# The low parts of a next batch's keys and values are formed by GpSimd instead of VectorE

## The chip, the cores and the metric

The kernel runs on one core of a Trainium2 chip. The metric is the device time of one execution in microseconds (us). A core has five engines that run side by side, each its own list of instructions in order, and wait for each other by semaphores: TensorE (PE in the profile, with PEld for its weight loads), VectorE (DVE), ScalarE (ACT), GpSimd (POOL) and SyncE (SP), which here only issues transfers (DMA).

## The reference

Two stages: an attention with squared ReLU in the place of a softmax, and a mixture of experts of which each token uses one.

```
scores = (1 / S) * z @ z.T                      # per batch: 2496 x 64 -> 2496 x 2496
attn   = max(scores, 0) ** 2
x      = u * (attn @ v)                         # v, u: 8 x 2496 x 256
...
do_compute = x @ w_skip > 0
xc     = x[do_compute]
logits = xc @ w_gate                            # 8 experts
e_idx  = argmax(logits)
gate_w = softmax(logits)[e_idx]
y      = gate_w * (max(xc @ w1[e_idx], 0) @ w2[e_idx])    # 256 -> 1024 -> 256
out    = x;  out[do_compute] = xc + y
```

All data are float32.

## The kernel before

**High and low parts.** TensorE multiplies in a rounded format (`F32R`). To keep the accuracy of float32 each factor is split: the high part is the rounded copy, the low part is what the rounding lost (`low = x - high`), and a product is three matmuls, high by high, high by low and low by high. So there are `zh`, `zl` for the queries and keys, `vh`, `vl` for the values, and `ah`, `al` for the squared scores.

**Loads.** `load_z` (L100) brings a tile `zf` of 128 x 512 of the transposed z by a DMA on SyncE, and returns a function that forms the parts: ScalarE casts `zh` (L108), and the engine that was passed in as `eng` subtracts for `zl` (L109). `load_v` (L113) does the same for a group of 256 rows of v: `raw`, then `vh` (L119) and `vl` (L120) of 128 x 512. There are four raw tiles, three `zf`, 35 tiles for `vh` and `vl` and seven each for `zh` and `zl`. A batch has ten groups of v and five tiles of z.

**Steps.** A batch is cut into five chunks of queries: four of 512 (`QC`) and a last of 448. For every chunk the loop goes through ten groups of 256 keys, in the order of `ORDER`. One (chunk, group) is a step; eight batches make 400 steps. `stage(s + LA)` with `LA` = 2 prepares the step two ahead: TensorE computes scores (L251), ScalarE applies ReLU (L292) and squares (L293), ScalarE or VectorE rounds to `ah` (L315), and VectorE subtracts for `al` (L319). Then `attend` (L346) multiplies `ah` and `al` with `vh` and `vl`, into accumulators `acc`. Because scores are symmetric, some tiles of squared scores are turned by VectorE (L268), kept in DRAM (`kept`) and read back in a later step in place of being computed again; in the last chunk such a tile comes as three pieces for `ah` and `al`.

At the end of a chunk VectorE adds and multiplies (L376, L379) and turns the result (L383), and it is stored. After every second chunk comes a routing: logits on TensorE (L414), on VectorE a series of small operations that choose the expert (L447 to L456), count the tokens (L460 to L468) and later form the places (L487 to L503), and on GpSimd indirect DMAs that scatter the tokens' ids into lists (L505).

**Order.** The order on every engine is written out by hand: `at(s, f)` puts `f` behind the work of step `s // 2` (so `s` counts half steps), and `later(s, k, load, ...)` starts the transfer at `s` and forms the parts `k` half steps later. While batch b is computed, `jobs` places the loads of batch b + 1: each entry is (function, group, chunk, position in the chunk), the transfer starts 3.5 steps before the position.

**The experts.** After the attention, weights are loaded in the same way by `load_w`; for all experts but the first the subtractions run on GpSimd already (L151, L157). Tokens are fetched by indirect DMAs (L556), multiplied, and put out (L654).

Of the kernel before, what the change touches and what calls it, by code (L numbers as in the profile page):

```python
# [47 lines left out]
def attn_moe(ctx, tc, zT, uT, v, wg, w1, w2, cst, pad, out):  # L48
# [4 lines left out]
    nc = tc.nc  # L53
# [3 lines left out]
    NB = v.shape[2]  # L57
# [105 lines left out]
    def load_u(ci):  # L163
        b, q0, n = chunks[ci]
        uts[ci] = xp.tile([P, 2, QC], F32, name="ut", tag="ut", bufs=3)
        nc.sync.dma_start(uts[ci][:, :, :n], uT[b, :, :, q0 : q0 + n])
# [509 lines left out]
    def at(s, f):  # L676

        todo.setdefault(s // 2, []).append(f)
# [24 lines left out]
    def later(s, k, load, *args):  # L703
        def start():
            f = load(*args)
            at(s + k, f)
        at(s, start)

    for ci, (b, q0, n) in enumerate(chunks):
        s0 = ci * NB  # L710
        if ci + 1 < NC:
            at(s0 + 12, lambda ci=ci: load_u(ci + 1))
        if ci == 0:
            first = [(4 * j - 8, j % 2, 3, load_z, j) for j in range(2, NZ)]
            first += [(2 * g - 4, 1, 4, load_v, g) for g in range(2, NB // 2)]
            for s1, _, k, load, j in sorted(first, key=lambda x: x[:2]):
                eng = nc.vector
                if s1 - k < 0:
                    at(s1, load(0, j, eng))
                else:  # L720
                    later(s1 - k, k, load, 0, j, eng)
            at(14, lay_pads)
        if q0 == 0 and b + 1 < B:

            jobs = [(load_v, 0, 1, 3), (load_z, 0, 1, 6), (load_v, 1, 2, 3), (load_z, 1, 2, 5), (load_v, 2, 2, 7)]
            jobs += [(load_v, 3, 3, 3), (load_v, 4, 3, 4), (load_v, 5, 3, 6), (load_v, 6, 3, 7)]
            jobs += [(load_v, 7, 4, 2), (load_z, 2, 4, 3), (load_v, 8, 4, 4), (load_z, 3, 4, 5)]
            jobs += [(load_v, 9, 4, 6), (load_z, 4, 4, 7)]
            for load, j, c, k in jobs:
                later(s0 + c * NB + 2 * k - 7, 7, load, b + 1, j, nc.vector)  # L730

    s_end = NC * NB
    s_w = s_end - 3 * NB
# [27 lines left out]
    for s, (ci, p) in enumerate(steps):  # L761
        b, q0, n = chunks[ci]
        k = s % NP
# [252 lines left out]
```

## Time and profile before

| | |
|---|---|
| time, median of 3 runs | 1785.65 us (1785.43 to 1788.15) |
| profiled execution, its time | 1782.95 us |
| profiled execution, its span | 1781.2 us |
| clock granted to TensorE | 0.999 |
| busy: TensorE, weight loads | 1760.8 us, 1555.9 us |
| busy: VectorE, ScalarE, GpSimd | 1185.5 us, 1159.5 us, 446.9 us |

A span goes from the first to the last instruction. A busy time is the union of an engine's instructions in the trace. The attention takes the span's first 1280 us or so, the experts the rest. Rows of a group read: line, engine, operation, written tile <- read tiles, shapes, count, then busy us and mean ns of one, then the engine's idle time just before these instructions and what ended it. Rows in order of time read: start us, length us, engine, line, operation, tiles, shapes, count; in brackets is idle time before it and what ended it.

### The profile page before, as it was taken

What the parts mean: (1) busy time and instruction counts of PE and PEld (TensorE: products, weight loads), DVE (VectorE), ACT (ScalarE), POOL (GpSimd) and SP (SyncE); (2) the same over time, 40 slices, a digit from 0 to 9 for tenths busy, and PEclk for the clock granted to TensorE, in tenths of its full rate; (3) what the DMA queues carried; (4) which work ended last, traced back from release to release, by engine and by line L of the source; (5) the groups of instructions that cost most, each with busy time, mean ns of one, the idle gap of its engine ahead of it and who ended that gap; (6) DMA issues with size and microseconds to landing.
All of it is one profiled execution on the core that took longest, in us unless ns stands there. A gap on an engine that the chain in (4) does not pass through costs nothing.

```text
span 1781.2 us, 40579 instructions
## 1 busy us (share of the span) xinstructions
PE 1760.8 (99%) x15844; PEld 1555.9 (87%) x15844; DVE 1185.5 (67%) x2113; ACT 1159.5 (65%) x1499; POOL 446.9 (25%) x421
## 2 busy tenths in 40 slices
PE   8999999999999999999999999999999999999997
PEld 6879878987887898788889888888999999999997
DVE  6877877787887787788778778777753433343332
ACT  8878877877788777778777877877633333333321
POOL 0102201211220120121112022012255556635621
PEclk9999999999999999999999999999999999999999
DMA  5476689478857947894794789488652323313210
GB/s 190 125 181 151 158 211 223 98 200 220 177 140 193 230 104 195 213 211 109 199 219 117 189 206 222 112 191 196 158 120 76 91 84 110 95 52 90 87 38 26
DMA packets 403763, 267.44 MB, mean 150 GB/s; under 512 B 205859, under 2 KB 334117, under 8 KB 403440
## 3 DMA queue, kind: packets, MB, share of 16 engines
q1 hardware_dynamic: 389440, 240.47, 55.2%
q0 software_dynamic: 13712, 22.99, 4.6%
q8 instruction: 141, 2.31, 0.6%
q14 instruction: 182, 1.49, 0.3%
q10 hardware_dynamic: 288, 0.17, 0.0%
HBM read 145.80 MB, written 118.39 MB: 148 GB/s over the span
## 4 chain that ended last, share of the span: by engine, by line
PE 86%; DMA 4%; ACT 3%; DVE 3%; issue 2%; SPq 1%; POOL 0%; DVEq 0%; POOLq 0%; ACTq 0%
PE acc L346 52%; PE psh L605 11%; PE y L624 11%; PE ps L251 10%; DMA out<-o,idt 2%; DVE al L319 2%; DMA r<-kept 1%; ACT ah L315 1%; PE psm L414 1%; SPq L280 1%; ACT r L292 1%; ACT r L293 1%; PE pst L574 1%; DVE rt L268 0%; DMA xr<-xrow 0%
## 5 line engine op out<-in xcount | busy, mean ns | idle before, releaser
L346 PE MATMUL acc<-ah,vh 64*128 64x512 f32 (+1 forms) x3120 | 661.6, 385 | 1.3 <-DVE ah L315 1.1
L346 PE MATMUL acc<-ah,vl 64*128 64x512 f32 (+1 forms) x3120 | 644.0, 383 | 0.0
L319 DVE TENSOR_TENSOR al<-r,ah 128x1024 fp32r<-128x1024 f32 (+3 forms) x464 | 479.1, 1048 | 190.9 <-ACT ah L315 181.1
L346 PE MATMUL acc<-al,vh 64*128 64x512 f32 (+1 forms) x3120 | 514.1, 385 | 1.5 <-DVE al L319 0.9
L505 POOL DMA_INDIRECT lst<-pair,dest x160 | 198.0, 1238 | 1052.1 <-DVE dest L503 952.4
L346 PEld LDWEIGHTS acc<-ah,vh 64*128 64x128 f32 x3120 | 347.2, 184 | 56.5 <-ACT ah L315 2.8
L292 ACT ACTIVATE r<-ps 128x1024 f32<-128x1024 f32 (+1 forms) x278 | 280.1, 1007 | 178.9 <-PE ps L251 170.0
L346 PEld LDWEIGHTS acc<-ah,vl 64*128 64x128 f32 x3120 | 346.0, 184 | 50.3 <-DVE vl L120 0.2
L346 PEld LDWEIGHTS acc<-al,vh 64*128 64x128 f32 x3120 | 320.8, 184 | 59.0 <-DVE al L319 10.9
L315 ACT CAST ah<-r 128x1024 fp32r<-128x1024 f32 (+3 forms) x381 | 330.4, 892 | 51.2 <-PE acc L346 38.3
L293 ACT ACTIVATE r<-r 128x1024 f32<-128x1024 f32 (+1 forms) x278 | 289.9, 1043 | 8.8
L610 ACT ACTIVATE hh<-psh 128x512 fp32r<-128x512 f32 (+1 forms) x172 | 98.8, 583 | 286.8 <-PE psh L605 246.6
L605 PE MATMUL psh<-xt,w1h 128*128 128x256 f32 (+1 forms) x1280 | 235.1, 285 | 2.3 <-issue 1.8
L624 PE MATMUL y<-w2t,hh 128*128 128x256 f32 x1328 | 235.9, 281 | 0.0
L611 DVE SCALAR_TENSOR_TENSOR hl<-psh,hh 128x512 fp32r<-128x512 f32 (+1 forms) x172 | 113.0, 670 | 137.2 <-ACT hh L610 129.3
L624 PEld LDWEIGHTS y<-w2t,hh 128*128 128x128 f32 x1328 | 202.3, 189 | 0.6 <-issue 0.6
L605 PEld LDWEIGHTS psh<-xt,w1h 128*128 128x128 f32 x1280 | 197.4, 189 | 3.2 <-issue 3.2
L624 PE MATMUL y<-w2t,hl 128*128 128x256 f32 x664 | 184.7, 278 | 1.3 <-DVE hl L611 1.3
L605 PE MATMUL psh<-xt,w1l 128*128 128x256 f32 (+1 forms) x640 | 181.9, 284 | 0.0
L268 DVE STREAM_TRANSPOSE rt<-r 128x512 f32<-128x512 f32 x244 | 158.3, 686 | 1.6 <-DMA kept<-rt 1.5
L251 PE MATMUL ps<-zh 64*128 64x512 f32 (+1 forms) x556 | 126.0, 398 | 4.8 <-ACT zh L108 4.8
L624 PEld LDWEIGHTS y<-w2t,hl 128*128 128x128 f32 x664 | 124.7, 188 | 1.6 <-DVE hl L611 1.5
(170 smaller groups left out, 1610.3 us busy)
## 6 DMA issues: line engine op xcount, KB each, us to landing
kept<-rt SPq DMA_DIRECT2D x244, 256.0 KB
r<-kept SPq DMA_DIRECT2D x488, 128.0 KB
raw<-in_v SPq DMA_DIRECT2D x80, 256.0 KB
ut<-in_uT SPq DMA_DIRECT2D x32, 512.0 KB
xr<-xrow SPq DMA_DIRECT2D x128, 128.0 KB
out<-xrow SPq DMA_DIRECT2D x128, 128.0 KB
raw<-in_w SPq DMA_DIRECT2D x64, 256.0 KB
zf<-in_zT SPq DMA_DIRECT2D x40, 256.0 KB
```

Of the source, the lines that this page charges most:

```text
L251: nc.tensor.matmul(to, k[h, o : o + P], queries(q, h, n), start=(m == 0), stop=(m == 2))
L268: nc.vector.transpose(t[:, :, 32 * k : 32 * k + 32], r[:, x, :].rearrange("p (m i) -> p m i", i=32))
L292: nc.scalar.activation(r[:, :, :n], ps[:, :, :n], AF.Relu, scale=isc)
L293: nc.scalar.activation(r[:, :, :n], r[:, :, :n], AF.Square)
L315: (nc.scalar.copy if on_act(ci, p) else nc.vector.tensor_copy)(h_, r_)
L319: nc.vector.tensor_sub(l_, r_, f32(h_))
L346: nc.tensor.matmul(acc[t][:, :n], w[h, x, dd], a[h, x, :n], start=(first and t not in halves[:m]), stop=(last and t not in halves[m + 1 :]),)
L505: put = nc.gpsimd.indirect_dma_start(out=lst, out_offset=bass.IndirectOffsetOnAxis(ap=dest[:, t : t + 1], axis=0), in_=pair[:, t, :], in_o ...
L605: nc.tensor.matmul(ps[:, j * W : (j + 1) * W], wt[:, a, o : o + P], x[:, d, :W], start=(m == 0), stop=(m == 5),)
L610: nc.scalar.activation(hh[:, : G * W], ps[:, : G * W], AF.Relu)
L611: nc.vector.scalar_tensor_tensor(hl[:, : G * W], ps[:, : G * W], 0.0, f32(hh[:, : G * W]), op0=ALU.max, op1=ALU.subtract)
L624: nc.tensor.matmul(ys[t], h[:, tt], w2t[f][:, k, :], start=(f == 0 and m == 0 and t % 2 == 0), stop=(f == NF - 1 and m == 2), skip_group_c ...
```

## The change

In `jobs`, the loads of the next batch's z and v, the engine that subtracts is `nc.gpsimd` in place of `nc.vector`:

```diff
@@ -727,7 +727,7 @@
             jobs += [(load_v, 7, 4, 2), (load_z, 2, 4, 3), (load_v, 8, 4, 4), (load_z, 3, 4, 5)]
             jobs += [(load_v, 9, 4, 6), (load_z, 4, 4, 7)]
             for load, j, c, k in jobs:
-                later(s0 + c * NB + 2 * k - 7, 7, load, b + 1, j, nc.vector)
+                later(s0 + c * NB + 2 * k - 7, 7, load, b + 1, j, nc.gpsimd)
```

The casts to `zh` and `vh` stay on ScalarE and the transfers on SyncE, at the same steps. The first batch's loads and the first expert's weights keep VectorE. So 7 x 10 subtractions for `vl` and 7 x 5 for `zl` change their engine, at the same places of the written order.

## The prediction

> **What bounds the kernel now.** I read the page's head first, then the waits of TensorE, then the groups by shape, and last the order of time around the places where TensorE waits. The page:
>
> ```profile
> span 1781.2 us, 40579 instructions
> PE 1760.8 (99%) x15844; PEld 1555.9 (87%) x15844; DVE 1185.5 (67%) x2113; ACT 1159.5 (65%) x1499; POOL 446.9 (25%) x421
> DVE  6877877787887787788778778777753433343332
> POOL 0102201211220120121112022012255556635621
> ```
>
> The first row is the span, the second the busy time of each engine, the other two the busy tenths of VectorE and GpSimd in 40 slices of 44.5 us. TensorE is busy 99% of the span. The attention fills the first 28 to 29 slices; there VectorE is at 70 to 80% and GpSimd at 0 to 20%. So there is room to move work into, but room on VectorE is worth only what TensorE waits for it. That is in the waits of TensorE (who waited, for what, total us, times, longest):
>
> ```profile
> PEld acc L346 <- DVE al L319: 10.9, 24, 0.6
> PE acc L346 <- DVE al L319: 0.9, 5, 0.2
> ```
>
> The weight loads of the second product waited 10.9 us in all for `al`, the matmuls themselves 0.9 us. No cure of VectorE can return more than about 10.9 us, 0.6% of the span, and most of it lies inside time in which earlier matmuls still ran.
>
> **The change part by part.** It moves 7 x 15 = 105 subtractions (ten `vl`, five `zl` for each of the batches b+1 = 1 to 7, formed during b = 0 to 6) from VectorE to GpSimd. Their groups, and the like group on GpSimd from the later part of the kernel:
>
> ```profile
> L120 DVE TENSOR_TENSOR vl<-raw,vh 128x512 fp32r<-128x512 f32 x80 | 54.0, 676 | 1.5 <-ACT vh L119 1.5
> L109 DVE TENSOR_TENSOR zl<-zf,zh 128x512 fp32r<-128x512 f32 x40 | 27.3, 681 | 3.9 <-ACT zh L108 3.9
> L151 POOL TENSOR_TENSOR w1l<-raw,w1h 128x512 fp32r<-128x512 f32 x24 | 30.9, 1298 | 0.5
> ```
>
> Removed from VectorE: 105 x 0.68 = 71 us busy. Added on GpSimd: 105 x 1.30 = 136 us, in the attention, where it is mostly idle. By length alone all of this is hidden: the casts on ScalarE and the DMAs of SyncE keep their places, and the last `zl` of a batch (step 47 of 50) is first read by the scores staged in step 52, five steps of 3.2 us (1281 / 400) later, so a GpSimd that is some us late costs nothing. Queued behind a `vl` on GpSimd are only scatters into `lst` (L505), which nothing reads before the last chunk, while the last moved load is in step 347 of 400. The raw tile comes free for the next transfer up to about 1 us later; four buffers with a reuse distance of five steps cover that.
>
> What is not hidden is the meeting of GpSimd and VectorE. These rows (start, length) show it:
>
> ```profile
> 280.26 0.97 POOL L505 DMA_INDIRECT lst<-pair,dest  x1 [0.30 <-issue]
> 401.79 1.69 POOL L505 DMA_INDIRECT lst<-pair,dest  x1 [2.51 <-DVE dest L503]
> 401.42 1.22 DVE L319 TENSOR_TENSOR al<-r,ah 128x1024 fp32r<-128x1024 f32 x1
> 390.98 1.71 POOL L505 DMA_INDIRECT lst<-pair,dest  x1 [47.08 <-DVE dest L503]
> 392.36 0.84 DVE L315 CAST ah<-r 128x1024 fp32r<-128x1024 f32 x1
> ```
>
> A scatter with VectorE idle takes 0.97 us. The one that starts at 401.79, inside an `al`, takes 1.69: the `al` ends at 402.64, 0.85 us after the scatter's start, and 0.85 + 0.84 = 1.69. So GpSimd stands still until VectorE's subtraction of two SBUF tensors is over, and then gets in. The other way round the trace has little: the `ah` at 392.36, begun under a scatter, took 0.84. No instruction of GpSimd that streams 512 elements meets an `al` in this trace. **The unknown price** is how long an `al` stands behind a subtraction on GpSimd: between nothing and the whole 1.30 us. I take the whole, since the same two engines exclude each other in the rows above with GpSimd as the loser. Since 1.30 is more than the 0.60 by which a removed subtraction lets the next instruction start earlier (447.79 to 448.39 below), VectorE gains where GpSimd runs beside transposes, and loses where it cuts into `al` or the routing.
>
> [...]
>
> Now the places. For nearly all loads the cast ends under an `al` that two transposes follow; GpSimd then starts at the `al`'s end and is through after 1.30 us, beside 1.3 us of transposes: no cost. Three places differ.
>
> *Place 1, chunk 4 of b = 1, 3, 5,* where seven loads, a routing and `al` in three pieces meet. ScalarE's casts, VectorE's order, and TensorE's use of `al`:
>
> ```profile
> 630.10 0.62 ACT L108 CAST zh<-zf 128x512 fp32r<-128x512 f32 x1
> 632.74 0.60 ACT L119 CAST vh<-raw 128x512 fp32r<-128x512 f32 x1
> 637.15 0.62 ACT L108 CAST zh<-zf 128x512 fp32r<-128x512 f32 x1
> 639.49 0.60 ACT L119 CAST vh<-raw 128x512 fp32r<-128x512 f32 x1
> 642.53 0.60 ACT L108 CAST zh<-zf 128x512 fp32r<-128x512 f32 x1
> ...
> 630.13 1.19 DVE L319 TENSOR_TENSOR al<-r,ah 128x384 fp32r<-128x384 f32 x3
> 632.25 0.17 DVE L453 SCALAR_TENSOR_TENSOR rm<-lg,rm 128x8 f32<-128x8 f32 x1
> 634.70 0.68 DVE L109 TENSOR_TENSOR zl<-zf,zh 128x512 fp32r<-128x512 f32 x1
> 635.30 1.22 DVE L319 TENSOR_TENSOR al<-r,ah 128x384 fp32r<-128x384 f32 x3
> 636.44 0.68 DVE L120 TENSOR_TENSOR vl<-raw,vh 128x512 fp32r<-128x512 f32 x1
> 639.81 0.69 DVE L109 TENSOR_TENSOR zl<-zf,zh 128x512 fp32r<-128x512 f32 x1
> 642.15 0.69 DVE L120 TENSOR_TENSOR vl<-raw,vh 128x512 fp32r<-128x512 f32 x1
> 643.63 1.09 DVE L319 TENSOR_TENSOR al<-r,ah 128x896 fp32r<-128x896 f32 x1
> ...
> 638.09 0.76 PE L346 MATMUL acc<-al,vh 64*128 64x448 f32 x4
> 645.28 0.55 PE L346 MATMUL acc<-al,vh 64*128 64x448 f32 x2
> ```
>
> The cast that ends at 630.72 lets GpSimd in between two pieces of the `al` of 630.13: its last piece waits 1.30, and so does all that follows. The cast that ends at 633.34 falls into the routing: GpSimd runs from 633.4 to 634.7, and the small two-input operation of L453, due at 632.25 + 1.30 = 633.55, waits 1.15. The `zl` of 634.70 is gone, 0.60: so far 1.30 + 1.15 - 0.60 = 1.85 late, and the `al` of 635.30 ends at 635.30 + 1.22 + 1.85 = 638.37, where TensorE wants it at 638.09. Then the lows of 636.44, 639.81 and 642.15 are gone (-1.80), and the casts that end at 637.77, 640.09 and 643.13 bring in GpSimd three more times (up to +3.90; +2.60 if one falls beside work that doesn't contend). The last `al` of the batch is thus late by 1.85 - 1.80 + 2.60 to 3.90 = 2.65 to 3.95. It ended at 643.63 + 1.09 = 644.72 for a use at 645.28, 0.56 ahead. So TensorE is 2.1 to 3.4 us later at the end of such a batch. I take 2.2, near the lower end, because a late cast moves its collision too. Three times: **+6.6 us**.
>
> *Place 2, the chunk after the routing of even b.* Rows of ScalarE, VectorE, TensorE:
>
> ```profile
> 446.47 0.60 ACT L119 CAST vh<-raw 128x512 fp32r<-128x512 f32 x1
> 447.26 0.16 DVE L464 TENSOR_TENSOR run_cnt<-pre,hot 128x8 bf16<-128x8 bf16 x1
> 447.79 0.68 DVE L120 TENSOR_TENSOR vl<-raw,vh 128x512 fp32r<-128x512 f32 x1
> 448.39 1.22 DVE L319 TENSOR_TENSOR al<-r,ah 128x1024 fp32r<-128x1024 f32 x1
> 449.66 0.30 PEld L346 LDWEIGHTS acc<-al,vh 64*128 64x128 f32 x4 [0.60 <-DVE al L319]
> 449.66 0.73 PE L346 MATMUL acc<-al,vh 64*128 64x512 f32 x4 [0.17 <-DVE al L319]
> ```
>
> Here TensorE already waits for `al`. The cast ends at 447.07, so GpSimd runs to 448.4, and the counting that should end at 447.42 waits about 1.15; the `vl` no longer stands ahead of `al` (it was formed long before), -0.60. Net +0.55 at b = 0, 2, 4, 6: **+2.2 us**. Without the wait it would be a gain of 0.2 to 0.6 each.
>
> *Place 3, the routing of odd b.* There the `vl` ahead of `al` was ready long before and GpSimd forms it early beside transposes:
>
> ```profile
> 576.08 0.69 DVE L120 TENSOR_TENSOR vl<-raw,vh 128x512 fp32r<-128x512 f32 x1
> 577.95 0.30 PEld L346 LDWEIGHTS acc<-al,vh 64*128 64x128 f32 x4 [0.65 <-DVE al L319]
> 577.95 0.74 PE L346 MATMUL acc<-al,vh 64*128 64x512 f32 x4 [0.21 <-DVE al L319]
> ```
>
> `al` comes 0.60 earlier and the stall (0.21 by the matmul, 0.65 by the weight load) goes; next is `ah` of the following step, not late. I take 0.4 at b = 1, 3, 5: **-1.2 us**.
>
> Sum: 6.6 + 2.2 - 1.2 = **+7.6 us** on the span of 1781.2, so 1788.8 (and 1790.6 for the profiled run, which took 1782.95). The median before is 1785.65, 2.7 above that run; I put the difference on the median: **1793.3 us**, +0.43%.
>
> **The rivals.** *A: VectorE does not wait for GpSimd* (the price's lower end). Then all three places only gain: 4 x 0.2 to 0.6 and 3 x 0.2 to 0.65, some 2.5 us less, **1783.2 us**. It isn't slower, and it decides where an `al` that begins under GpSimd keeps its 1.22 us. For it: no wait of VectorE on GpSimd is in the trace. Against: GpSimd's wait on VectorE is. It could pass 0.2% only if most of the 10.9 us went. *B: the wait is there but short,* because the collisions fall beside transposes more often than I counted or the claim is given up between parts: place 1 costs 1 us or less, the rest cancels: +1.5, **1787 us**. *C: the wait is whole and the delays build up,* place 1 at 3.4 us, place 2 at 0.9, and some 1 us in chunk 4 of each of four even batches, where seven loads also meet pieces of `al`: 10.2 + 3.6 + 4 - 1.2 = +16.6, **1802 us**.
>
> **How the numbers follow.** Forecast 50%, A 22%, B 18%, C 10%. Its own range is +4 to +12: 1789.5 to 1798. The range for 8 in 10 takes in A and B and leaves out most of C: 1783 to 1799. A measurement of this kernel tells about 0.2% (3.6 us) from no change. Slower by more: nearly all of the forecast and C, a little of B: 0.58. Faster by more: a corner of A: 0.05. The rest, 0.37, is within.
>
> **What would show it.** Right: `al` (L319) rows well over 1.22 us or started late right under a GpSimd subtraction, subtractions on GpSimd of up to 2.5 us, TensorE's waits on `al` growing from 10.9 us with new ones at the end of chunk 4 of odd b, and the wait at the routing of odd b gone. Wrong: `al` unchanged at 1.22 us beside GpSimd (then A), or collisions there but TensorE's waits not grown, so that the lead of two steps covers them (then B). A slower matmul at the same waits would mean a cause that I haven't priced.

## The result, and the profile after

The changed kernel takes 1797.48 us (median of 4 runs, 1794.9 to 1799.59), the one before, timed beside it, 1786.9 (1785.43 to 1788.42). The ratio is 1.0067, with a 95% interval of 1.0055 to 1.0079: slower by 0.67%. Forecast was 1793.3 us, +0.43%.

The page after, span and busy times:

```profile
span 1793.0 us, 40679 instructions
PE 1763.8 (98%) x15844; PEld 1564.2 (87%) x15844; DVE 1180.6 (66%) x2008; ACT 1159.9 (65%) x1499; POOL 609.7 (34%) x526
```

The span is 11.8 us longer. Two numbers tell the story at once. GpSimd is busy 163 us more (446.9 to 609.7), though 105 instructions of 1.30 us are only 136. VectorE is busy only 5 us less (1185.5 to 1180.6), though 105 instructions of 0.68 us, 71 us, have left it. Both engines have grown by waiting inside their instructions. The groups by shape show where:

```profile
L120 POOL TENSOR_TENSOR vl<-raw,vh 128x512 fp32r<-128x512 f32 x70 | 105.5, 1507 | 437.1 <-ACT vh L119 302.5 <-DMA xr<-xrow 111.3 <-DMA r<-kept 23.1
L109 POOL TENSOR_TENSOR zl<-zf,zh 128x512 fp32r<-128x512 f32 x35 | 52.4, 1497 | 61.2 <-ACT zh L108 52.3 <-DMA out<-xrow 4.4 <-DMA r<-kept 4.2
L319 DVE TENSOR_TENSOR al<-r,ah 128x896 fp32r<-128x896 f32 x48 | 67.6, 1408 | 9.9 <-ACT ah L315 4.3 <-PE acc L346 1.0 <-DVE ah L315 0.5
L319 DVE TENSOR_TENSOR al<-r,ah 128x384 fp32r<-128x384 f32 x64 | 53.2, 871 | 1.4 <-ACT ah L315 1.0
```

A subtraction on GpSimd takes 1.50 us on the mean, 0.2 more than the like one in the experts' part (1.30). The `al` of the last chunks of a batch, 128x896 and 128x384, take 1.41 and 0.87 us on the mean, where they took 1.09 and 0.54 before:

```profile
L319 DVE TENSOR_TENSOR al<-r,ah 128x896 fp32r<-128x896 f32 x48 | 52.4, 1092 | 9.5 <-ACT ah L315 4.8 <-DVE ah L315 0.5
L319 DVE TENSOR_TENSOR al<-r,ah 128x384 fp32r<-128x384 f32 x64 | 32.0, 540 | 1.6 <-ACT ah L315 1.5
```

TensorE's waits (who, for what, total us, times, longest):

```profile
PEld acc L346 <- DVE al L319: 23.4, 36, 1.9
PE acc L346 <- DVE al L319: 9.7, 12, 1.5
```

The weight loads wait 12.5 us more for `al` than before (10.9), the matmuls 8.8 us more (0.9); the span's 11.8 us lie between the two. (The medians of the timed runs differ by 10.6 us.)

To see where, I took from both traces, for each of the 400 steps, the start of the first matmul of L346 that reads the step's `al`, and looked at where the distance between the two traces grows. At the end of the attention it is 11.75 us, so the experts' part has lost nothing. It grows at few steps:

```
place                                               after - before, us
1  chunk 4 of b = 1, 3, 5 (steps 46 to 49)          2.01 + 2.01 + 2.03 = +6.05
2  routing of b = 0, 2, 4, 6 (step 36)              0.42 + 0.14 + 1.41 + 0.14 = +2.11
3  routing of b = 1, 3, 5 (steps 26, 27)            -0.31 - 0.38 - 0.38 = -1.07
-  chunk 4 of b = 0, 2, 4, 6 (steps 45, 49)         0.64 + 0.63 + 0.64 + 0.88 = +2.79
-  start of chunk 3 of b = 1 (step 30)              +1.39
-  all others, each under 0.25                      +0.48
```

Place 1, at b = 3, in order of time (GpSimd, VectorE, TensorE):

```profile
635.59 1.66 POOL L109 TENSOR_TENSOR zl<-zf,zh 128x512 fp32r<-128x512 f32 x1 [2.11 <-ACT zh L108]
638.67 1.33 POOL L120 TENSOR_TENSOR vl<-raw,vh 128x512 fp32r<-128x512 f32 x1 [1.42 <-ACT vh L119]
647.65 0.98 POOL L505 DMA_INDIRECT lst<-pair,dest  x1 [0.30 <-issue]
648.66 1.30 POOL L109 TENSOR_TENSOR zl<-zf,zh 128x512 fp32r<-128x512 f32 x1
649.91 1.29 POOL L120 TENSOR_TENSOR vl<-raw,vh 128x512 fp32r<-128x512 f32 x1
...
635.12 2.29 DVE L319 TENSOR_TENSOR al<-r,ah 128x384 fp32r<-128x384 f32 x3
638.88 2.32 DVE L462 TENSOR_TENSOR pre<-pre,hot 128x8 bf16<-128x8 bf16 x7
648.45 3.70 DVE L319 TENSOR_TENSOR al<-r,ah 128x896 fp32r<-128x896 f32 x1
...
652.21 0.66 PE L346 MATMUL acc<-al,vh 64*128 64x448 f32 x3 [1.52 <-DVE al L319]
```

The `al` of 635.12 is that of 630.13 before: its three pieces take 2.29 us in place of 1.19. Then, in the routing, the seven additions of the counting (x7) take 2.32 us, in place of 1.35. The last collision is the largest: an `al` that takes 1.09 us alone takes 3.70, because two subtractions of GpSimd, without a gap between them, lie over it from 648.66 to 651.20; they had stood in GpSimd's queue behind the scatter of 647.65. TensorE stands for 1.52 us.

Places 2 (at b = 2, then at b = 4) and 3 (at b = 3):

```profile
451.38 1.29 POOL L120 TENSOR_TENSOR vl<-raw,vh 128x512 fp32r<-128x512 f32 x1 [4.08 <-ACT vh L119]
451.50 1.20 DVE L464 TENSOR_TENSOR run_cnt<-pre,hot 128x8 bf16<-128x8 bf16 x1
454.03 0.73 PE L346 MATMUL acc<-al,vh 64*128 64x512 f32 x4 [0.31 <-DVE al L319]
...
771.86 1.30 POOL L120 TENSOR_TENSOR vl<-raw,vh 128x512 fp32r<-128x512 f32 x1 [2.94 <-ACT vh L119]
771.48 2.48 DVE L462 TENSOR_TENSOR pre<-pre,hot 128x8 bf16<-128x8 bf16 x7
774.01 0.21 PE L481 MATMUL psm<-pre,ones 64*128 64x64 bf16 x2 [0.61 <-DVE pre L462]
775.79 0.74 PE L346 MATMUL acc<-al,vh 64*128 64x512 f32 x4 [0.79 <-DVE al L319]
...
582.81 0.30 PEld L346 LDWEIGHTS acc<-al,vh 64*128 64x128 f32 x4 [0.23 <-DVE al L319]
```

At 451.50 an addition over eight columns, 0.16 us alone, takes 1.20 beside GpSimd. There only that last addition stood behind GpSimd. At b = 4 GpSimd began 0.38 us after the first of the seven additions (771.48), so they took 2.48 us; the matmuls of L481, which read the counts, waited 0.61 us, `al` came later too, and the step lost 1.41 in place of 0.14 us. In place 3 the weight load's wait is 0.23 us, where it was 0.65.

Chunk 4 of an even b, and the one step at b = 1 that I hadn't seen coming:

```profile
475.69 1.31 POOL L120 TENSOR_TENSOR vl<-raw,vh 128x512 fp32r<-128x512 f32 x1
480.74 1.32 POOL L109 TENSOR_TENSOR zl<-zf,zh 128x512 fp32r<-128x512 f32 x1 [0.92 <-ACT zh L108]
475.37 7.11 DVE L319 TENSOR_TENSOR al<-r,ah 128x384 fp32r<-128x384 f32 x5
480.50 0.69 PE L346 MATMUL acc<-al,vh 64*128 64x448 f32 x4 [0.46 <-DVE al L319]
...
272.15 1.30 POOL L120 TENSOR_TENSOR vl<-raw,vh 128x512 fp32r<-128x512 f32 x1
271.99 3.70 DVE L319 TENSOR_TENSOR al<-r,ah 128x1024 fp32r<-128x1024 f32 x2 [0.26 <-ACT ah L315]
274.61 0.73 PE L346 MATMUL acc<-al,vh 64*128 64x512 f32 x4 [1.40 <-DVE al L319]
```

Five pieces of `al` that need some 0.4 us each (1.19 by three in the row of 630.13) take 7.11 us, while four subtractions run on GpSimd, of which the rows show the first, at 475.69, and the last, at 480.74. And two `al` of 1.22 us take 3.70.

### The profile page after: what moved, and what is told of

Its sections match the earlier page's. It is cut to its first block, busy times and chain, and to the rows that moved or that the text cites. A ratio compares the mean times of both kernels' runs of the same rounds, so it can differ in the third digit from the quotient of the medians.

```text
span 1793.0 us, 40679 instructions
## 1 busy us (share of the span) xinstructions
PE 1763.8 (98%) x15844; PEld 1564.2 (87%) x15844; DVE 1180.6 (66%) x2008; ACT 1159.9 (65%) x1499; POOL 609.7 (34%) x526
## 5 line engine op out<-in xcount | busy, mean ns | idle before, releaser
L319 DVE TENSOR_TENSOR al<-r,ah 128x1024 fp32r<-128x1024 f32 (+3 forms) x464 | 522.1, 1142 | 204.1 <-ACT ah L315 192.8
L346 PE MATMUL acc<-ah,vh 64*128 64x512 f32 (+1 forms) x3120 | 642.4, 385 | 0.8 <-DVE ah L315 0.6
L346 PE MATMUL acc<-ah,vl 64*128 64x512 f32 (+1 forms) x3120 | 627.2, 383 | 0.0
L346 PE MATMUL acc<-al,vh 64*128 64x512 f32 (+1 forms) x3120 | 497.7, 385 | 10.3 <-DVE al L319 9.7
L346 PEld LDWEIGHTS acc<-ah,vh 64*128 64x128 f32 x3120 | 325.6, 184 | 54.2 <-ACT ah L315 2.8
L346 PEld LDWEIGHTS acc<-ah,vl 64*128 64x128 f32 x3120 | 326.2, 184 | 47.9 <-DVE vl L120 0.2
L346 PEld LDWEIGHTS acc<-al,vh 64*128 64x128 f32 x3120 | 307.3, 184 | 68.3 <-DVE al L319 23.4
L505 POOL DMA_INDIRECT lst<-pair,dest x160 | 203.5, 1272 | 404.3 <-DVE dest L503 361.4
L120 POOL TENSOR_TENSOR vl<-raw,vh 128x512 fp32r<-128x512 f32 x70 | 105.5, 1507 | 437.1 <-ACT vh L119 302.5
L654 POOL DMA_INDIRECT out<-o,idt x77 | 77.0, 1000 | 169.9 <-DVE o L653 147.4
```

What stands on the lines that cost most here:

```text
L120: eng.tensor_sub(vl, vf, f32(vh))
L319: nc.vector.tensor_sub(l_, r_, f32(h_))
L346: nc.tensor.matmul(acc[t][:, :n], w[h, x, dd], a[h, x, :n], start=(first and t not in halves[:m]), stop=(last and t not in halves[m + 1 :]),)
L505: put = nc.gpsimd.indirect_dma_start(out=lst, out_offset=bass.IndirectOffsetOnAxis(ap=dest[:, t : t + 1], axis=0), in_=pair[:, t, :], in_o ...
```

## The experiments

The theory, drawn from the rows above (an `al` of 1.09 us that took 3.70, an addition of 0.16 us that took 1.20): an instruction of VectorE with two inputs in SBUF and one of GpSimd that reads SBUF don't run at the same time; what the change costs is VectorE waiting for GpSimd, where an `al` is needed soon. Rival 1: the lows now come later, or free their raw tiles later, and that is what is waited for. Rival 2: any work of GpSimd on SBUF holds VectorE up. Ratios are against the kernel before, timed beside each run.

**Side reads.** VectorE keeps its subtractions, and GpSimd gets a reading with no purpose, at the place in its order that the change uses. Its result goes to `scr`, the space of the experts' tiles `idt`, which the three runs with a scratch allocate as one tile:

```diff
...
-            at(s + k, f)
+            b = args[0]
+
+            def g():
+                f()
+                hi = f32((vt if load is load_v else zt)[args[:2]][0])
+                h = hi.rearrange("p a d -> p (a d)") if load is load_v else hi
+                for q in (0, 256):
+                    nc.gpsimd.tensor_sub(scr, h[:, q : q + 256], h[:, q : q + 256])
+
+            at(s + k, g if b else f)
```

> VectorE keeps the low parts, as before the change; GpSimd, which has nothing to deliver here, subtracts two halves of the same high part (2 x 128x256, some 1.48 us) at the same place of its order, into a scratch tile that nothing reads. Theory (an instruction of VectorE with two SBUF inputs waits until a GpSimd instruction that reads SBUF is over): the collisions come without the relief of 0.60 us each, so more than the change cost: +25 to +55 us on the span of 1781.2, and al rows of over 2 us. Rival 1 (the change is slow because the low parts come later, or their raw tiles are freed later): the low parts are as early as before, so 0 to +2 us and al rows as before.

Measured: 1799.33 us, ratio 1.0087 (1.007 to 1.0104), span +15.7 us. The instructions of GpSimd (min/median/max ns) and of VectorE (the same) in that run:

```profile
L715 POOL TENSOR_TENSOR idt<-vh x140: 607/819/1510, 59.4 to 1133.4; 128x256 f32<-128x256 f32 x140
L319 DVE TENSOR_TENSOR al<-r,ah x464: 279/1221/1646, 9.8 to 1295.2; 128x1024 fp32r<-128x1024 f32 x107, 128x384 fp32r<-128x384 f32 x24, 128x896 fp32r<-128x896 f32 x16, 128x128 fp32r<-128x128 f32 x8
```

Rival 1 isn't needed for the loss: the lows were formed by VectorE as before, and the kernel lost more than with the change. Nor does the profile of the changed kernel show it: no wait of TensorE ends on a `vl` or `zl` of GpSimd, and the transfers wait for its `vl` 1.2 us in all. The size was missed: I expected 25 us and more, with `al` over 2 us, and no `al` took more than 1.65. The halves took only 0.61 us where nothing met them, not 0.74, and VectorE got in between two of them (the two from 157.13 us took 2.03 us in all, beside three pieces of `al` that took 2.47 from 157.73, where such three take 1.19 alone). (In this profile the clock granted to TensorE is 0.50 from 977.6 to 981.0 us, and the step there is 1.67 us longer than before; by the medians the run costs 15.5 us.)

**The same as one instruction.** To see whether that explains the miss, the two halves became one instruction (its result bf16, to fit the scratch):

```diff
-                for q in (0, 256):
-                    nc.gpsimd.tensor_sub(scr, h[:, q : q + 256], h[:, q : q + 256])
+                nc.gpsimd.tensor_sub(scr, h, h)
```

> The side reads again (VectorE keeps the low parts, GpSimd's result is read by nobody), but as one instruction of 128x512 in place of two halves. Theory (a collision costs what is left of one GpSimd instruction): more than the two halves' +15.7 us, +20 to +40 us, with al rows of up to 1.22 + 1.3 us. Rival (what counts is GpSimd's reading in all, however it is cut): +13 to +18 us, like the halves.

Measured: 1806.61 us, ratio 1.0124 (1.0108 to 1.0139), span +23.2 us. The groups, in the same form:

```profile
L714 POOL TENSOR_TENSOR idt<-vh x70: 1034/1110/1557, 60.7 to 1139.6; 128x512 bf16<-128x512 f32 x70
L319 DVE TENSOR_TENSOR al<-r,ah x464: 275/1218/2748, 9.9 to 1302.5; 128x1024 fp32r<-128x1024 f32 x107, 128x384 fp32r<-128x384 f32 x24, 128x896 fp32r<-128x896 f32 x16, 128x128 fp32r<-128x128 f32 x8
```

The reading in all is shorter (1.03 us against 2 x 0.61) and costs more: 21.7 us against 15.5 by the medians. So the rival, which had 13 to 18 us, fails: the length of the single instruction counts. (That its result is bf16 was not tried apart.)

**Side writes.** In the place of the two halves, GpSimd copies one column and fills the scratch four times:

```diff
-                for q in (0, 256):
-                    nc.gpsimd.tensor_sub(scr, h[:, q : q + 256], h[:, q : q + 256])
+                nc.gpsimd.tensor_copy(scr[:, :1], h[:, :1])
+                for _ in range(4):
+                    nc.gpsimd.memset(scr, 0.0)
```

> As the run with side reads, but GpSimd reads only one column and then fills the scratch tile four times (4 x 128x256, some 1.2 us), which reads nothing. Theory (it is the read that excludes): the one column takes some 0.1 us, so 0 to +3 us, al rows of 1.22 us. Rival 2 (any work of GpSimd on SBUF holds VectorE up): like the side reads, +20 to +50 us. Rival 1: 0 to +2 us.

Measured: 1783.4 us, ratio 1.0 (0.9991 to 1.001), and the attention ends 0.2 us earlier than before.

```profile
L716 POOL MEMSET idt<- 128x256 f32 x420 | 133.9, 319 | 24.3
L319 DVE TENSOR_TENSOR al<-r,ah x464: 280/1219/1228, 9.8 to 1279.1; 128x1024 fp32r<-128x1024 f32 x107, 128x384 fp32r<-128x384 f32 x24, 128x896 fp32r<-128x896 f32 x16, 128x128 fp32r<-128x128 f32 x8
```

GpSimd is as busy as with the change (4 x 0.32 us a load), and not one `al` takes longer than 1.23 us, though 62 of them begin under a fill. Rival 2 is out: it isn't any work on SBUF. What the subtractions do and the fills don't is to read SBUF. The copies of one column (min/median/max ns), which do read, bear it out from the other side:

```profile
L714 POOL COPY idt<-zh x35: 183/496/877, 73.4 to 1119.2; 128x1 f32<-128x1 f32 x35
```

Alone a copy takes 0.18 us, not the 0.1 that I expected; where it begins under an `al` it stands until some 0.04 us behind the `al`'s end.

**By part.** Either the loads of chunk 4 go back to VectorE, or they alone go to GpSimd:

```diff
-                later(s0 + c * NB + 2 * k - 7, 7, load, b + 1, j, nc.vector)
+                later(s0 + c * NB + 2 * k - 7, 7, load, b + 1, j, nc.vector if c == 4 else nc.gpsimd)
...
+                later(s0 + c * NB + 2 * k - 7, 7, load, b + 1, j, nc.gpsimd if c == 4 else nc.vector)
```

> The changed kernel, but the six loads of chunk 4 keep VectorE. Theory: the steps that lost time in chunk 4 of the changed kernel (3 x 2.02 us for odd b, 2.8 us for even b together) are whole again, the rest stays: +3 us on the span (+1 to +4.5). Rival 1 (lateness of the low parts, the same for each load): 6 of 15 loads less, 11.8 x 9/15 = +7 us.

> The other part alone: only the six loads of chunk 4 are on GpSimd. Theory: +9 us (+7.5 to +10.5), nearly all of it in steps 45 to 49 of a batch. Rival 1: 11.8 x 6/15 = +4.7 us, spread.

Measured: chunk 4 on VectorE 1785.15 us, ratio 1.0006 (0.9996 to 1.0015); chunk 4 alone on GpSimd 1792.52 us, ratio 1.0051 (1.0033 to 1.007). The theory's +3 and +9 are met (the medians differ by 1.3 and 8.7 us, the spans by 3.5 and 8.6), the rival's +7 and +4.7 are not. By the steps, the attention ends 2.46 us later than before without chunk 4 (1.35 of it in the first two steps, ahead of any moved load) and 9.50 us later with chunk 4 alone:

```
place                              both     without chunk 4    chunk 4 alone
1  chunk 4 of odd b               +6.05            0              +5.96
2  routing of even b              +2.11          +0.84              0
3  routing of odd b               -1.07          -1.07              0
-  chunk 4 of even b              +2.79            0              +2.66
-  step 30 of b = 1               +1.39          +1.39              0
```

Each place has its own cost and loses or keeps it with its own loads. The one difference, place 2, is b = 4, where the step lost 0.13 us in place of 1.41. Six of the fifteen loads of a batch cost 9.5 of the 11.75 us, so it isn't a price for each load.

**Two halves.** The changed kernel, with each subtraction on GpSimd cut in two, so that VectorE might get in between:

```diff
-            eng.tensor_sub(vl, vf, f32(vh))
+            for a in (slice(0, 1), slice(1, 2)) if b else (slice(0, 2),):
+                eng.tensor_sub(vl[:, a, :], vf[:, a, :], f32(vh[:, a, :]))
```

(and `zl` in the same way).

> The changed kernel with each subtraction on GpSimd cut into two of 128x256 (0.74 us each by the w2t rows), which depend on nothing of each other. Theory as the changed kernel's 3.70 us al suggests (GpSimd instructions that stand ready one behind the other leave VectorE no gap): the two halves hold as one of some 1.48 us, so the same cost or a little more, +11 to +17 us on the span, al rows up to 1.22 + 1.5 us and more. Theory as the side reads suggest (VectorE gets in between two halves): a collision costs at most 0.74 us, so about half, +4 to +8 us, and no al over 2.1 us.

Measured: 1792.94 us, ratio 1.0046 (1.0031 to 1.0061), 8.0 us by the medians. In the profile the attention ends 9.8 us later than before, but 1.67 of it fall in one step in which the granted clock is 0.50 (from 651.6 to 655.0 us). So the size is at the upper edge of the second theory's +4 to +8, while its `al` rows (none over 2.1 us) were missed; neither theory holds as a whole, and both things happen. In chunk 4 of even b the halves and the pieces of `al` take turns (at b = 0 five pieces from 154.57 us take 4.62 us, beside pairs of halves that take 1.79 to 2.12; with whole subtractions four pieces from 153.62 took 5.56), and the loss there, +2.79 us with whole subtractions, is gone. In place 1 they don't (GpSimd, then VectorE, at b = 1):

```profile
326.42 1.43 POOL L110 TENSOR_TENSOR zl<-zf,zh 128x256 fp32r<-128x256 f32 x2
327.81 1.41 POOL L122 TENSOR_TENSOR vl<-raw,vh 128x256 fp32r<-128x256 f32 x2
...
326.29 3.89 DVE L321 TENSOR_TENSOR al<-r,ah 128x896 fp32r<-128x896 f32 x1
```

One `al` of 1.09 us stands until all four halves are through, and place 1 costs as much as with whole subtractions (3 x 2.06 us). (Lines are two higher in this kernel.)

**Picked loads.** Last, a version that should gain from the same mechanism. One load of a batch goes to GpSimd: the one whose low stood ahead of a late `al`, and whose cast ends where VectorE goes on to transposes.

```diff
-                later(s0 + c * NB + 2 * k - 7, 7, load, b + 1, j, nc.vector)
+                eng = nc.gpsimd if load is load_v and j == (1 if b % 2 else 3) else nc.vector
+                later(s0 + c * NB + 2 * k - 7, 7, load, b + 1, j, eng)
```

> Before the change, but one load of a batch is on GpSimd: v group 1 in odd b, v group 3 in even b, the ones that stood ahead of a late al in places 2 and 3 and whose cast ends under transposes. Theory: GpSimd meets nothing, and the relief of 0.60 us is left: the seven waits of 0.60 to 0.65 us at the routing go, -2 to -3 us on the span of 1781.2 (0.1 to 0.2%). Rival 1 (each low part that is formed late costs the same): 11.8 x 7/105 = +0.8 us.

Measured: 1782.24 us (11 runs) against 1784.95 (15 runs), ratio 0.9984 (0.9975 to 0.9993): faster than the kernel before, by 0.16%, and so than the changed one. The waits of the weight loads for `al`:

```profile
PEld acc L346 <- DVE al L319: 7.3, 19, 0.6
```

They are 3.6 us less than before. From step 2 on the attention gains 2.6 us, -0.31, -0.38, -0.38 at place 3 and some -0.33 at place 2 of b = 2, 4, 6. (The profiled execution of this run has a span of 1784.5: its first two steps and its experts' part, which the edit doesn't touch, were 1.3 and 4.6 us longer than in the profile before. In the experts' part the granted clock is twice 0.50 for 3.4 us, from 1331.4 and from 1741.0 us; in the profile before it is so only at the very end. The timed runs don't show a loss.)

## Why the prediction was right, and where its size was off

*What bounds the kernel.* Right. TensorE was full, VectorE had little to give back: even with seven loads picked for gain, 0.16% came out.

*The unknown price.* Right: an `al` waits for the rest of a GpSimd subtraction, which reads SBUF. Ahead of the runs that was my estimate, since the trace before shows only GpSimd waiting (a scatter of 1.69 us in place of 0.97); the two runs with side reads show it for VectorE (`al` up to 1.65 and 2.75 us, spans +15.7 and +23.2 us). The upper end of 1.30 us was the right bound for a single collision (`al` of 128x1024 up to 2.56 us in the run without chunk 4, 1.22 + 1.34; the 24 `al` of the changed kernel that began behind a subtraction lost up to 1.12 us). It was no upper end where two GpSimd instructions stood one behind the other: 3.70 - 1.09 = 2.61 us. That such a pair leaves no gap I hadn't foreseen. Side writes show that it is not the writing that holds `al` up (ratio 1.0, no `al` over 1.23 us). The prediction counted a loss only where GpSimd's subtraction began first; by the starts that the trace shows, eight `al` of the changed kernel lost 1.34 to 2.78 us to subtractions that began after them (the last section has them).

*Place 1.* Forecast +6.6, measured +6.05. The first half of the course came as worked out: 1.10 us at the `al` of 630.13 and 0.97 in the routing (1.30 and 1.15 forecast), and little lost for TensorE at the `al` of 635.30 (0.33 us). The second half did not: not three collisions one by one, but a pair of subtractions that stood behind scatters on GpSimd and then ran together over the last `al` (1.68 us of the 2.01 at b = 3). That the sums come so close is in part luck. (The prediction speaks of seven loads in chunk 4; there are six.)

*Place 2.* Forecast +2.2, measured +2.11. But the four were not alike: 0.14 to 0.42 three times, 1.41 once. At b = 2 GpSimd's subtraction falls on the last of the small additions of the counting, at b = 4 on the first ones. Without chunk 4 the same loads cost 0.13 us at b = 4 and 0.84 in all, so that the sum came out at 2.1 is luck.

*Place 3.* Forecast -1.2, measured -1.07.

*What failed.* The three places sum to +7.1, close to the forecast's +7.6. The rest of the 11.8 is the step "For nearly all loads the cast ends under an `al` that two transposes follow ... no cost. Three places differ." It was not true of chunk 4 of even b (+2.79), where the six loads meet pieces of `al` as well; I priced it only in rival C, at 1 us for each. And at step 30 of b = 1 (+1.39) a `vl` on GpSimd, held up behind two scatters, fell on an `al`. Both show in the run by parts, as costs of their own. The term that was mis-sized is thus the loads counted as free: 0 by the forecast, +4.2 measured.

*The rivals.* A and B are out by the `al` of 3.70 us and by TensorE's waits. Of C, the cost of the even chunks came true in kind (2.79 us in place of 4), the longer places 1 and 2 did not.

## What to carry to other kernels

Before work is moved from VectorE to GpSimd, count where its reading will lie over two-input instructions of VectorE that something waits for: room by busy share (GpSimd 25%, VectorE 67% before) was no room here, where an `al` of 1.09 us took up to 3.70 beside GpSimd, and what counted was the length of GpSimd's instruction (1.30 us) against the lead of VectorE's result (0.56 us at place 1). Move only the instructions that fall beside work that isn't held up, here the transposes (0.686 us beside a subtraction, 0.687 without; casts of VectorE are held up too, the longest from 0.85 to 1.58 us, see below), and look at what else stands in GpSimd's queue, since a held-up pair fell on VectorE as one long block here (2.61 us at place 1). Where the first engine is full to 99%, look first at how much its waits can give back at all: here it was 10.9 of 1781 us.

## What the runs showed of the hardware that was not expected

- An `al` that started ahead of GpSimd's subtraction could still lose: the one of 648.45 began 0.21 us before GpSimd's at 648.66 and stood through it and the next one. In these cases GpSimd's instruction was ready behind a scatter that was just ending. In the profile before, a scatter that started 0.37 us after an `al` waited for it (401.79 after 401.42). The profile of the changed kernel sorts these cases cleanly: eight `al` lost 1.34 to 2.78 us to subtractions that began after them, and each had begun in the last 0.15 to 0.31 us of a scatter that had the subtraction right behind it. They stand at the end of place 1, in chunk 4 of even b and at step 30 of b = 1, and the steps that wait for them lose 8.4 of the 11.75 us (for the one at b = 6 nothing is lost). Where GpSimd's subtraction came out of idle, an `al` only 0.03 us ahead of it went through, and the subtraction waited (635.59, 1.66 us). A scatter alone held no `al` up: before the change 76 begin under a scatter, and the longest of them takes 1.23 us. What decides within those tenths of a microsecond was not tried.
- Halves and pieces take turns in one place and not in another (above); why was not tried either.
- The collision is in the length of the instruction, not in the idle time before it: nearly all of VectorE's 71 us of removed work came back as longer rows, so its busy share of 66% looks as if nothing had been removed.
- Transposes and casts of VectorE have one input each, but beside GpSimd's subtractions only the transposes keep their length (of the 244 to `rt`, 74 run beside a subtraction and take 0.686 us on the mean, the others 0.687). The longest cast to `ah` on VectorE grew from 0.85 to 1.58 us. Casts collide even with writing: in the run with side writes, all six fills that began under such a cast took 0.74 to 0.77 us in place of 0.31. After the change (the cast as min/median/max ns):

```profile
L268 DVE STREAM_TRANSPOSE rt<-r 128x512 f32<-128x512 f32 x244 | 158.3, 686 | 0.0
L315 DVE CAST ah<-r x83: 614/686/1583, 9.1 to 1290.3; 128x1024 fp32r<-128x1024 f32 x51, 128x896 fp32r<-128x896 f32 x32
```
